# Row divisions and copies on ScalarE for the first batches, sums for several chunks at once, and conversion of whole weight pieces

## The chip, the core and the metric

The kernel runs on one core of a Trainium2 chip. A core has five engines that run their own instruction streams in order and wait for each other by semaphores: TensorE (PE in the profile; its weight loads are PEld), VectorE (DVE), ScalarE (ACT), GpSimd (POOL) and SyncE (SP), which here issues every DMA. The metric is the time of one execution in microseconds on the device; the kernel before takes 2252.2 us (median of 3 runs, 2251.06 to 2255.11).

## The reference

Eight batches of attention, and then one block on the joined heads. For each batch and each of 12 heads (448 tokens, 64 numbers each):

```
q_n, k_n = rmsnorm(q, g_q), rmsnorm(k, g_k)
scores = q_n @ k_n.T / 8;  attn = exp(scores - max);  attn /= sum(attn) + 1e-9
x[:, 64*h : 64*h+64] = attn @ v                     # x: 448 x 768 per batch
u  = x + real(fft(fft(x, axis=tokens), axis=features))
un = (u - mean(u)) / sqrt(var(u) + 1e-6)
out = u + relu(un @ w_ch1) @ w_ch2                  # 768 -> 3072 -> 768
```

All is float32 but for the two weight matrices, which arrive as float64.

## The kernel before

**Stages.** `aux(b)` does the attention of batch b and its Fourier part, `ffn(b)` its feed-forward network (FFN). `aux(0)` runs alone; then, for b = 0 to 7, `ffn(b)` runs merged with `aux(b + 1)`. The generators yield costs and `merge` interleaves them; after that a scheduler of the tile framework settles each engine's order from its own model of the times, so that the order in the built program is not that of the code.

**Attention.** Two heads make a pair, six pairs a batch, and the 448 rows of a pair's scores are four chunks of 112. `softmax_pair` (L325) does for each chunk: scores on TensorE into two PSUM banks (L339 or L342), a minimum per row on VectorE (`mn`; the scores carry a minus sign), the exponential on ScalarE (`P`, with the sum of each row in `sm`), then on VectorE the small operations on `sm` (add 1e-9, reciprocal), and the division of P by its sums, one operation per head: on VectorE, but for head 0 of the first two batches (`EARLY` = 2), where ScalarE does it. `value_pair` (L370) turns P by TensorE transposes, a "remainder" first (`rem`, L374), then three blocks per head (`pt`, L386 or L417), evicts each block from PSUM (`T`) and multiplies it by v (`av`). For the six pairs of batch 0 (`PLAIN_PAIRS`) the eviction is one plain float32 copy, on VectorE and ScalarE in turn; for later pairs it is a split into two parts of the type float32r: ScalarE writes the high part, VectorE the rest. `av` ends in the tile `xT`.

**Fourier part.** `fold` (L472) adds and subtracts halves of xT on VectorE into `eo` and `tot`; matmuls with constant matrices give `y`, ScalarE and VectorE split it into `Y`, and so on up to `un`, whose transposes `unT` are the FFN's input. For batches 2 to 7 the three `eo` of a batch lie in slots of the tag X.

**FFN.** `up(m)` makes 128 of the 3072 hidden rows with 18 matmuls (L844, `h`), `down(g, d)` 128 of the 768 output rows with 12 (L865, `o`). ScalarE and VectorE evict `h` as two float32r parts (`hs`), VectorE adds `o` up in `acc`. Two PSUM banks with the tag ffn serve both.

**Weights.** The matrices come in 60 pieces: 24 of w1 (128 x 768 numbers) and 36 of w2 (128 x 512). Each is turned once from float64 into two float32r parts (`converted`, L682), kept in DRAM, and loaded from there for all later batches. 14 pieces are turned during `aux(0)` (`CONVERT_EARLY`; tiles w1e, w2e), the rest in the FFN of batch 0. `convert` (L632) takes half a piece at a time: a DMA into a raw tile `dbl` (tag X, four slots), two ScalarE operations (L643 `mag`, L644 `dbl`), three on VectorE (L645, L649, L653, all into `mag`), an addition on GpSimd (L657), a cast on ScalarE (L658, `w`) and a subtraction on GpSimd (L659). `mag` is a whole tile for the two halves (tag M, two slots). GpSimd also does the norms' squares, products and powers (`qkn`, `raw`, `ss`) for the early pairs.

`V`, `A` and `G` are recorders, so that most operations of VectorE, ScalarE and GpSimd have the line L111; they are told apart by their tiles.

## Time and profile before

| | |
|---|---|
| three runs | 2252.2, 2251.06, 2255.11 us |
| the profiled execution | 2245.9 us, of which the span from first to last instruction is 2244.1 |
| mean granted TensorE clock | 0.963 |
| TensorE busy (weight loads) | 2107.8 us, 94% (1851.1 us, 82%) |
| VectorE busy | 1636.7 us, 73% |
| ScalarE busy | 1074.1 us, 48% |
| GpSimd busy | 574.0 us, 26% |
| DMA | 425.37 MB, mean 190 GB/s |

The profile is one execution. "Busy" is the time in which an engine has an instruction under way; a matmul's end is modelled, so that a TensorE that is shown as busy all the time need not be at its peak. A row of a group reads: line, engine, operation, tile written <- tiles read, shapes, count | busy us in all, mean ns of one | idle us just before them, and who ended it. A row of the timeline reads: start, duration, engine, line, operation, tiles, shapes, count. The stages follow each other so: attention of batch 0 up to about 150 us, its Fourier part and the handoff to the FFN up to about 200 us, the FFN of batch 0 with the attention of batch 1 up to about 550 us, then the FFNs of batches 1 to 6, each with the attention of the next batch, up to 2000 us, and the last FFN alone.

### The profile page before, as it was taken

The numbers are of one execution on the slowest core, as the hardware profiler recorded it, in microseconds if no ns is written. First come the engines' busy times: TensorE is split into PE (matmuls) and PEld (weight loads), VectorE is DVE, ScalarE is ACT, GpSimd is POOL, SyncE is SP. The second block draws the span as 40 slices with busy tenths as digits, with TensorE's granted clock in tenths as the row PEclk, the third lists the DMA queues.
The fourth block names the chain that finished last, engine by engine and source line by source line (L and its number), as shares of the span: only waits on it lengthen the run. The fifth ranks groups of instructions, "written<-read, shape, count | busy, mean of one in ns | idle before, by whom it ended". The sixth has DMA issues, their size and how long they took to land.

```text
span 2244.1 us, 32060 instructions
## 1 busy us (share of the span) xinstructions
PE 2107.8 (94%) x11164; PEld 1851.1 (82%) x11164; DVE 1636.7 (73%) x3281; ACT 1074.1 (48%) x2452; POOL 574.0 (26%) x442
## 2 busy tenths in 40 slices
PE   6967986788999999999999999999999999999997
PEld 3336865667999999999999999999999999998997
DVE  6897899898688577876788587866788587753122
ACT  5856777475554255534554355524554355422100
POOL 5883567476122011210122021211121022000000
PEclk7997987899999999999999999999999999999999
DMA  5556555577755585556655575557655674539665
GB/s 137 174 167 210 171 171 163 173 266 256 218 174 169 184 238 165 180 182 207 200 171 177 193 222 169 173 177 225 187 171 177 207 215 161 177 132 279 212 215 136
DMA packets 299187, 425.37 MB, mean 190 GB/s; under 512 B 187489, under 2 KB 225362, under 8 KB 299026
## 3 DMA queue, kind: packets, MB, share of 16 engines
q1 hardware_dynamic: 299026, 423.32, 61.1%
q8 instruction: 89, 1.46, 0.3%
q14 instruction: 72, 0.59, 0.1%
HBM read 363.47 MB, written 65.27 MB: 191 GB/s over the span
## 4 chain that ended last, share of the span: by engine, by line
PE 76%; DVE 10%; issue 4%; DMA 3%; POOL 3%; ACT 2%; SPq 0%; DVEq 0%; POOLq 0%; ACTq 0%
PE h L844 28%; PE o L865 27%; PE S L342 5%; PE av L429 4%; PE pt L417 4%; PE y L520 1%; PE qk L305 1%; DVE magw L653 1%; DVE mn L111 1%; DMA dblw<-w 1%; POOL magw L657 1%; DVE magw L645 1%; PE oT L810 1%; DMA u_dram<-u 1%; DMA w<-w 1%
## 5 line engine op out<-in xcount | busy, mean ns | idle before, releaser
L865 PE MATMUL o<-hs,w 128*128 128x448 f32 x3456 | 801.0, 374 | 13.3 <-ACT w L658 4.4
L844 PE MATMUL h<-unT,w 128*128 128x448 f32 x3456 | 781.4, 371 | 3.3 <-DVE hs L111 3.3
L865 PEld LDWEIGHTS o<-hs,w 128*128 128x128 f32 x3456 | 643.9, 191 | 71.7 <-ACT w L658 5.8
L844 PEld LDWEIGHTS h<-unT,w 128*128 128x128 f32 x3456 | 640.5, 189 | 57.1 <-DVE hs L111 4.3
L111 ACT ACTIVATE P<-S,mn 112x448 f32<-112x448 f32 x384 | 243.1, 635 | 218.7 <-DVE mn L111 196.8
L111 POOL TENSOR_TENSOR qkn<-raw 112x1024 f32<-112x1024 f32 x47 | 90.4, 1924 | 740.4 <-PE qk L305 481.2
L111 DVE TENSOR_REDUCE mn<-S 112x1 f32<-112x448 f32 x384 | 232.9, 616 | 48.8 <-PE S L342 45.7
L111 ACT ACTIVATE hs<-h 128x448 fp32r<-128x448 f32 x192 | 104.4, 544 | 294.0 <-PE h L844 293.1
L111 DVE TENSOR_TENSOR acc<-o,acc 128x448 f32<-128x448 f32 x240 | 148.6, 620 | 106.9 <-PE o L865 105.2
L111 DVE SCALAR_TENSOR_TENSOR hs<-h,hs 128x448 fp32r<-128x448 f32 x192 | 119.2, 621 | 125.8 <-ACT hs L111 123.8
L429 PE MATMUL av<-T,vhl 128*128 128x448 f32 x504 | 181.5, 392 | 19.2 <-DVE T L111 12.5
L111 ACT CAST T<-pt 128x448 fp32r<-128x448 f32 x252 | 133.2, 532 | 133.9 <-PE pt L417 131.6
L111 DVE TENSOR_TENSOR T<-pt,T 128x448 fp32r<-128x448 f32 x252 | 154.9, 616 | 35.5 <-ACT T L111 34.0
L111 POOL TENSOR_TENSOR ss<-ss,nhalf 112x16 f32<-112x16 f32 x48 | 151.7, 3160 | 108.9 <-DVE ss L111 107.2
L111 DVE TENSOR_SCALAR P<-P,sm 112x448 f32<-112x448 f32 x336 | 159.5, 509 | 4.3
L342 PE MATMUL S<-KD,QT 128*112 128x448 f32 x352 | 142.6, 407 | 10.5 <-ACT P L111 5.2
L417 PE MATMUL pt<-ident,P 112*128 112x112 f32 x1008 | 147.0, 264 | 4.4 <-DVE R L111 2.8
L417 PEld LDWEIGHTS pt<-ident,P 112*128 112x128 f32 x1008 | 123.0, 143 | 25.7 <-DVE R L111 3.6
L111 POOL TENSOR_TENSOR rstd<-st,nhalf 112x1 f32<-112x1 f32 (+2 forms) x32 | 18.4, 575 | 487.5 <-DVE st L111 484.6
L342 PE MATMUL S<-KL,QT 128*112 128x448 f32 x352 | 134.7, 385 | 2.0 <-DVE KL L111 1.9
L429 PEld LDWEIGHTS av<-T,vhl 128*128 128x128 f32 x504 | 96.4, 192 | 32.0 <-DVE T L111 17.0
L657 POOL TENSOR_TENSOR magw<-magw,dblw 128x256 uint32<-128x256 uint32 (+1 forms) x92 | 87.4, 960 | 81.6 <-DVE magw L653 55.7
(121 smaller groups left out, 2680.3 us busy)
## 6 DMA issues: line engine op xcount, KB each, us to landing
w<-w SPq DMA_DIRECT2D x288, 512.0 KB, 4.3
w<-w SPq DMA_DIRECT2D x192, 768.0 KB, 4.5
dblw<-w SPq DMA_DIRECT2D x60, 256.0 KB, 3.0
dblw<-w SPq DMA_DIRECT2D x32, 384.0 KB, 3.9
raw<-q SPq DMA_DIRECT2D x96, 112.0 KB, 4.6
raw<-k SPq DMA_DIRECT2D x96, 112.0 KB, 3.7
v<-v SPq DMA_DIRECT2D x96, 96.0 KB, 3.6
u_dram<-u SPq DMA_DIRECT2D x24, 336.0 KB, 3.5
```

Of the source, the lines that this page charges most:

```text
L111: ins = emit(*args, **kwargs)
L305: nc.tensor.transpose(pt[:, c * C : (c + 1) * C], qk[:, i, c].rearrange("t h d -> t (h d)"), ident[:C, :C],)
L342: nc.tensor.matmul(s_, QT[:, h, cs], K[:, h], start=step == 0, stop=step == 1)
L417: nc.tensor.transpose(pt[:, c * C : (c + 1) * C], Pc[c][:, 512 * h + j * 128 : 512 * h + (j + 1) * 128], ident[:C, :C],)
L429: nc.tensor.matmul(av[:, :S], lv, T[:, i], start=(j == 0 and i == 0), stop=False)
L520: nc.tensor.matmul(o, src[:, par, t0 : t0 + n], D1[:, ri, par, cols], start=i != 1, stop=i != 0,)
L645: behind(nc.vector.tensor_scalar(out=value, in0=value, scalar1=MIN_HIGH, scalar2=MAX_HIGH, op0=ALU.max, op1=ALU.min,))
L653: behind(nc.vector.scalar_tensor_tensor(out=bits, in0=high, scalar=0xC0000000, in1=bits, op0=ALU.bitwise_and, op1=ALU.bitwise_or,))
L657: behind(nc.gpsimd.tensor_tensor(out=bits, in0=bits, in1=low, op=ALU.add))
L810: nc.tensor.transpose(op[:n, j * 128 : (j + 1) * 128], accs[b][:, 3 * half + j, t0 : t0 + n], ident,)
L844: pace(nc.tensor.matmul(o, w[:, a, c], unT[c][:, z], start=n == 0, stop=n == 17))
L865: pace(nc.tensor.matmul(o, w[:, a, f], hs[4 * g + f][:, z], start=n == 0, stop=n == 11))
```

## The change

Four edits.

1. *Early divisions.* For the first two batches ScalarE does the division for both heads; VectorE keeps those of batches 2 to 7.
2. *Sums of several chunks.* `sm` holds up to four chunks' sums. Adding 1e-9 and the reciprocal are done once for two chunks (batch 0) or four (later batches). The divisions of these chunks come after them, so four or eight in a row.
3. *Plain evictions.* All 36 copies `T` of batch 0 go to ScalarE, where VectorE had 18.
4. *Whole pieces.* `convert` is called once per piece, with a raw tile of 1800 words (two slots in place of four of 900), so each of its operations is twice as wide and there are half as many. Where `fold` used a slot of the tag X, two `eo` now share one wide tile.

```diff
--- before
+++ after
-    SLOTS = {"P": 8, "PT": 6, "X": 4, "M": 2, "unT": 6, "h": 6}
+    SLOTS = {"P": 8, "PT": 6, "M": 2, "unT": 6, "h": 6}
...
+    def wide(name, dtype=F32):
+        return sb.tile([128, 1800], dtype, tag="X", name=name, bufs=2)
...
     def softmax_pair(b, p, Pc):
+        together = 2 if b == 0 else NC
...
-            sm = sb.tile([C, 2], F32, tag="sm", name=f"sm{b}_{p}_{c}", bufs=4)
+            if c % together == 0:
+                sm = sb.tile([C, NC, 2], F32, tag="sm", name=f"sm{b}_{p}_{c}", bufs=2)
...
-                    accum_out=sm[:, h : h + 1],
-                )
-            V.tensor_scalar(
-                out=sm, in0=sm, scalar1=1e-9, scalar2=None, op0=ALU.add
-            )
-            V.reciprocal(sm, sm)
-            for h in range(2):
-                if b < EARLY and h == 0:
-                    A.activation(Ph[h], Ph[h], AF.Copy, scale=sm[:, h : h + 1])
-                    continue
-                V.tensor_scalar(
-                    out=Ph[h], in0=Ph[h], scalar1=sm[:, h : h + 1], scalar2=None,
-                    op0=ALU.mult,
+                    accum_out=sm[:, c % together, h : h + 1],
                 )
             Pc.append(P)
             yield 760
+            if (c + 1) % together:
+                continue
+            sums = sm[:, :together]
+            V.tensor_scalar(
+                out=sums, in0=sums, scalar1=1e-9, scalar2=None, op0=ALU.add
+            )
+            V.reciprocal(sums, sums)
+            for n, P in enumerate(Pc[c + 1 - together : c + 1]):
+                for h in range(2):
+                    ph = P[:, h * S : (h + 1) * S]
+                    if b < EARLY:
+                        A.activation(ph, ph, AF.Copy, scale=sums[:, n, h : h + 1])
+                    else:
+                        V.tensor_scalar(
+                            out=ph, in0=ph, scalar1=sums[:, n, h : h + 1], scalar2=None,
+                            op0=ALU.mult,
+                        )
...
-                    if (h * 3 + j) % 2 == 0:
-                        V.tensor_copy(T, pt[:, :S])
-                    else:
-                        A.copy(T, pt[:, :S])
+                    A.copy(T, pt[:, :S])
...
-        eo = slot(kept, f"eo{b}_{p}").rearrange("r (i t) -> r i t", i=2)
+        if kept is not None:
+            eo = slot(kept, f"eo{b}_{p}")
+        else:
+            if p % 2 == 0:
+                halves[b] = wide(f"eo{b}_{p}")
+            eo = halves[b][:, p % 2 * 900 : p % 2 * 900 + 900]
+        eo = eo.rearrange("r (i t) -> r i t", i=2)
...
-        raw = slot("X", f"dbl{name}", U32)[:, : c * f].rearrange(
+        raw = wide(f"dbl{name}", U32)[:, : c * f].rearrange(
...
-            for c in (slice(0, self.n // 2), slice(self.n // 2, self.n)):
-                convert(
-                    src[:, c], bits[:, c], [hl[:, k, c] for k in range(2)],
-                    f"{self.tag}{name}_{c.start}",
-                )
+            convert(src, bits, [hl[:, k] for k in range(2)], f"{self.tag}{name}")
```

What this does to the order of the instructions, at two places. First VectorE in the steady part, at the end of the last pair (5) of batch 3; a tile's name has batch, pair and chunk (`P3_5_2`: batch 3, pair 5, chunk 2), o2 and acc2 belong to the FFN of batch 2. Before:

```order
L111 TENSOR_REDUCE mn3_5_3_9629<-S3_5_3_0_9631 112x1
L111 TENSOR_REDUCE mn3_5_3_9629<-S3_5_3_1_9632 112x1
L111 TENSOR_TENSOR acc2_7837<-o2_3_0_9645,acc2_7837 128x448
L111 TENSOR_SCALAR sm3_5_3_9630<-sm3_5_3_9630 112x2
L111 RECIPROCAL sm3_5_3_9630<-sm3_5_3_9630 112x2
L111 TENSOR_SCALAR P3_5_3_9628<-P3_5_3_9628,sm3_5_3_9630 112x448 x2
L111 TENSOR_TENSOR T3_4_1_1_9666<-pt3_4_1_1_9661,T3_4_1_1_9666 128x448
L111 TENSOR_TENSOR acc2_7837<-o2_3_1_9671,acc2_7837 128x448
```

And now:

```order
L111 TENSOR_REDUCE mn3_5_3_8825<-S3_5_3_1_8827 112x1
L111 TENSOR_TENSOR acc2_7092<-o2_3_1_8862,acc2_7092 128x448
L111 TENSOR_SCALAR sm3_5_0_8603<-sm3_5_0_8603 112x8
L111 RECIPROCAL sm3_5_0_8603<-sm3_5_0_8603 112x8
L111 TENSOR_SCALAR P3_5_0_8601<-P3_5_0_8601,sm3_5_0_8603 112x448
L111 TENSOR_TENSOR T3_4_1_2_8883<-pt3_4_1_2_8878,T3_4_1_2_8883 128x448
L111 TENSOR_SCALAR P3_5_0_8601<-P3_5_0_8601,sm3_5_0_8603 112x448
L111 TENSOR_SCALAR P3_5_1_8683<-P3_5_1_8683,sm3_5_0_8603 112x448 x2
L111 TENSOR_SCALAR P3_5_2_8763<-P3_5_2_8763,sm3_5_0_8603 112x448 x2
L111 TENSOR_TENSOR KL_66<-qk4_0_1_8888,KD4_0_8814 64x448
L111 TENSOR_SCALAR P3_5_3_8824<-P3_5_3_8824,sm3_5_0_8603 112x448 x2
```

Before, only the last chunk's two divisions come after its minimum, since those of the chunks ahead have been done; now all eight do, and with them work of the FFN (`acc2`) and of the pair ahead (`T3_4`, `KL`) stands among them. On TensorE the order has 27 to 54 matmuls of the FFN between a pair's last scores and the first transpose of its P in batches 3 to 7 (24 to 44 before), and 30 or more in batch 2.

Then ScalarE at the handoff from `aux(0)` to the FFN: `xT0` is the attention's output of batch 0, `xr0` a copy of part of it, `w1e5` and `w1e6` casts of early weight pieces, `dblw2_6` a step of a later piece that waits for its load, `Y0` the evictions of the Fourier part. Before:

```order
L111 COPY xr0_0_1546<-xT0_136 128x6x112
L111 COPY xr0_0_1546<-xT0_136 128x6
L658 CAST w1e5_1379<-magw1e5_1380 128x384 x2
L658 CAST w1e6_1468<-magw1e6_1469 128x384 x2
L111 CAST Y0_0_0_1498<-y0_0_0_1491 113x390
L644 ACTIVATE dblw2_6_0_2205<-dblw2_6_0_2205 128x256
L111 CAST Y0_0_1_1508<-y0_0_1_1501 112x390
L644 ACTIVATE dblw2_6_2_2215<-dblw2_6_2_2215 128x256
L111 CAST Y0_1_0_1518<-y0_1_0_1511 113x390
L111 CAST Y0_1_1_1528<-y0_1_1_1521 112x390
```

And now:

```order
L111 COPY xT0_136<-av0_5_0_1246 64x448
L673 CAST w1e5_1233<-magw1e5_1234 128x768
L111 COPY xT0_136<-av0_5_1_1273 64x448
L111 COPY xT0_136<-xT0_136 128x1
L111 COPY xr0_0_1380<-xT0_136 128x6x112
L111 COPY xr0_0_1380<-xT0_136 128x6
L111 CAST Y0_0_0_1332<-y0_0_0_1325 113x390
L673 CAST w1e6_1312<-magw1e6_1313 128x768
L111 CAST Y0_0_1_1342<-y0_0_1_1335 112x390
L111 CAST Y0_1_0_1352<-y0_1_0_1345 113x390
L111 CAST Y0_1_1_1362<-y0_1_1_1355 112x390
L659 ACTIVATE dblw2_6_2001<-dblw2_6_2001 128x512
```

The cast of `w1e5` has moved from behind both `xr0` copies to between the two last `xT0` copies, that of `w1e6` stands behind the first `Y0`, and the steps of `dblw2_6` no longer stand between the `Y0`. Elsewhere in `aux(0)` and `aux(1)` the order has 48 + 48 divisions on ScalarE (24 + 24 before) and none on VectorE, and 13 of the 14 early pieces pass ScalarE ahead of the first `Y0`, as before.

More of the change, by code (lines that the diff above doesn't have):

```diff
@@ L191, in spectral_block @@
     X_BANKS = (("either", "either"), ("either", "either"))
-    FOLD_SLOTS = (("unT", "unT"), ("PT", "P"), ("M", "X"))
+    FOLD_SLOTS = (("unT", "unT"), ("PT", "P"), ("M", None))
     loaded = {}
@@ L470, in spectral_block @@
     rstds = {}
+    halves = {}
     def fold(b, p, xT, EO):
```

## The prediction

> **What bounds the kernel now.** I read the table by stages first, for which engine is full where, then the chain of waits, then the groups of instructions in the stages that are not full of matmuls. Columns: stretch, length, then busy time of each engine with its count of instructions, granted clock, DMA share, GB/s.
>
> ```profile
> core 0: us, PE busy (x) PEld busy (x) DVE busy (x) ACT busy (x) POOL busy (x), PEclk, DMA share, GB/s
> 25.00:150.00 125.00, 103.84 (x404) 44.84 (x404) 115.98 (x246) 101.99 (x256) 99.52 (x74) 0.91 0.55 165
> 150.00:200.00 50.00, 28.26 (x125) 21.87 (x126) 40.43 (x82) 24.90 (x56) 26.16 (x21) 0.62 0.62 192
> 200.00:250.00 50.00, 50.00 (x277) 45.46 (x276) 35.95 (x73) 36.17 (x84) 20.97 (x18) 1.00 0.51 166
> 250.00:450.00 200.00, 153.71 (x716) 128.60 (x715) 188.78 (x359) 135.22 (x320) 128.37 (x112) 0.83 0.54 173
> 450.00:550.00 100.00, 83.67 (x387) 69.68 (x386) 93.93 (x197) 65.93 (x164) 70.13 (x84) 0.91 0.80 272
> 550.00:2000.00 1450.00, 1448.07 (x8086) 1326.64 (x8086) 1089.74 (x2198) 673.47 (x1510) 219.01 (x122) 1.00 0.62 188
> 2000.00:2244.00 244.00, 227.54 (x1152) 207.96 (x1150) 63.08 (x120) 31.31 (x58) 2.19 (x4) 0.97 0.66 202
> ```
>
> From 550 to 2000 us TensorE is busy 1448 of 1450 us at clock 1.00: only fewer matmuls would shorten it, and the change removes none. The last 244 us hold the last FFN, which the change does not touch. What can move is the first 550 us, where TensorE is not full and its clock falls to 0.83. There VectorE is the full one: 116.0 of 125 us (93%), and 188.8 of 200 (94%). In 450-550 us the DMA engines are busy too (0.80, in one slice 0.86).
>
> ```profile
> PE 76%; DVE 10%; issue 4%; DMA 3%; POOL 3%; ACT 2%; SPq 0%; DVEq 0%; POOLq 0%; ACTq 0%
> 475.00:500.00 25.00, 21.02 (x104) 17.83 (x103) 24.86 (x53) 19.06 (x44) 17.17 (x20) 0.93 0.86 300
> POOL magw L657 <- DVE magw L653: 52.6, 38, 4.3
> ACT dblw L644 <- DMA dblw<-w: 24.6, 21, 4.0
> ```
>
> The chain's 10% on VectorE is 224 us; after 550 us TensorE leaves no room for it. The last two rows are waits between 250 and 550 us: GpSimd waits for VectorE in the conversion, ScalarE for its loads.
>
> **Attention of batch 0 (25-150 us).** VectorE loses its half of the 48 divisions, the 18 evictions and half of the sums' small operations:
>
> ```profile
> L111 DVE TENSOR_SCALAR P<-P,sm 112x448 f32<-112x448 f32 x24 | 17.5, 731 | 0.2
> L111 DVE TENSOR_SCALAR sm<-sm 112x2 f32<-112x2 f32 x24 | 13.1, 547 | 0.0
> L111 DVE COPY T<-pt 128x448 f32<-128x448 f32 x18 | 11.1, 615 | 4.2 <-PE pt L386 4.1
> L111 DVE RECIPROCAL sm<-sm 112x2 f32<-112x2 f32 x24 | 3.7, 154 | 0.1
> ```
>
> That is 17.5 + 11.1 + (13.1 + 3.7)/2 = 37.0 us, so VectorE falls to about 79. ScalarE takes the work over. Its rows of the same operations, and two of the conversion (from 250-450 us):
>
> ```profile
> L111 ACT ACTIVATE P<-P,sm 112x448 f32<-112x448 f32 x24 | 16.1, 672 | 4.0 <-DVE sm L111 3.9
> L111 ACT COPY T<-pt 128x448 f32<-128x448 f32 x18 | 9.5, 529 | 0.1
> L644 ACT ACTIVATE dblw<-dblw 128x384 uint32<-128x384 uint32 x22 | 12.2, 557 | 9.9 <-DMA dblw<-w 9.7
> L644 ACT ACTIVATE dblw<-dblw 128x256 uint32<-128x256 uint32 x26 | 11.1, 435 | 8.3 <-DMA dblw<-w 8.2
> ```
>
> It gains 16.1 + 9.5 us. A whole piece saves it one start per operation: 128 elements cost 557 - 435 = 122 ns, so a whole 512 takes 679 ns where two halves take 870; the 768 saves the same 191 ns. Three operations for each of the 13 pieces that the order has in this stage: 7.4 us. ScalarE comes to 102.0 + 25.6 - 7.4 = 120.2 of 125 us and takes VectorE's place as the full engine. Full without a gap it would allow 120 us (-5); at 85% (TensorE has 83% here now, ScalarE 82%), 141 (+16). I take the 93% that VectorE reaches: 120.2/0.928 = 129.5, **+4 us**.
>
> **The handoff (150-200 us).** Every engine is partly idle; ScalarE by 25 us, in a queue where conversion casts stand ahead of the Y copies. The order puts one cast ahead of the xT copy now and takes a load's wait from between the Y copies. A gain and a loss are both possible; **0**, with 6 us either way (an estimate: a quarter of that idle time). **200-250 us** is full of matmuls: **0**.
>
> **FFN of batch 0 with attention of batch 1 (250-450 us).**
>
> ```profile
> L645 DVE TENSOR_SCALAR magw<-magw 128x384 f32<-128x384 f32 x22 | 14.4, 674 | 0.7 <-ACT magw L643 0.5
> L653 DVE SCALAR_TENSOR_TENSOR magw<-dblw,magw 128x384 uint32<-128x384 uint32 x24 | 14.0, 594 | 0.0
> L111 DVE TENSOR_SCALAR P<-P,sm 112x448 f32<-112x448 f32 x16 | 13.3, 831 | 0.1
> L649 DVE TENSOR_SCALAR magw<-magw 128x256 uint32<-128x256 uint32 x26 | 13.1, 520 | 0.0
> L653 DVE SCALAR_TENSOR_TENSOR magw<-dblw,magw 128x256 uint32<-128x256 uint32 x24 | 12.3, 531 | 0.0
> L649 DVE TENSOR_SCALAR magw<-magw 128x384 uint32<-128x384 uint32 x24 | 12.0, 515 | 0.0
> L645 DVE TENSOR_SCALAR magw<-magw 128x256 f32<-128x256 f32 x26 | 9.2, 371 | 1.1 <-ACT magw L643 1.0
> L111 DVE TENSOR_SCALAR sm<-sm 112x2 f32<-112x2 f32 x16 | 5.2, 324 | 0.0
> ```
>
> The divisions are 13.3 us. The sums are 5.2 us, with reciprocals 16 x 154 ns = 2.5; four chunks at once leave a quarter: -5.8. The six conversion rows make 75.0 us. What of that is work and what is waiting, single rows of the timeline show (VectorE, then two of GpSimd):
>
> ```profile
> 322.26 0.28 DVE L649 TENSOR_SCALAR magw<-magw 128x256 uint32<-128x256 uint32 x1
> 323.40 0.41 DVE L653 SCALAR_TENSOR_TENSOR magw<-dblw,magw 128x256 uint32<-128x256 uint32 x1
> 343.45 0.43 DVE L111 TENSOR_SCALAR P<-P,sm 112x448 f32<-112x448 f32 x1
> 344.73 0.34 DVE L649 TENSOR_SCALAR magw<-magw 128x384 uint32<-128x384 uint32 x1
> 345.52 0.54 DVE L653 SCALAR_TENSOR_TENSOR magw<-dblw,magw 128x384 uint32<-128x384 uint32 x1
> 347.82 3.01 DVE L111 TENSOR_SCALAR P<-P,sm 112x448 f32<-112x448 f32 x1
> 346.64 2.01 POOL L657 TENSOR_TENSOR magw<-magw,dblw 128x384 uint32<-128x384 uint32 x2
> 348.61 1.98 POOL L659 TENSOR_TENSOR w<-magw,w 128x384 fp32r<-128x384 f32 x2
> ```
>
> One division takes 0.43 us, the next 3.01: it ends at 350.83, just as GpSimd's run of four ends at 350.59. The Trainium skill (SBUF — State Buffer, Who interferes with whom) states this as a rule: such a VectorE operation and a GpSimd one share a port pair, and the second waits for the whole instruction of the first. This trace agrees.
>
> Free, three half operations take 0.28 x 2 + 0.41 = 0.97 us (256) or 1.22 us (384). Here some 12.7 pieces of the first and 11.7 of the second kind are 53 us of work and 22 of waiting. By the step from 256 to 384 a whole piece costs 0.40 x 2 + 0.67 = 1.47 or 0.52 x 2 + 0.93 = 1.97 us free: 42 us. Half as many instructions that each wait as long as now add 11: saved 22. If the waits stay 22, 11 is saved; if they go, 33. By the skill's rule each instruction of GpSimd, twice as long, would hold the port twice as long, so the saving would be the 11.
>
> VectorE: 188.8 - 13.3 - 5.8 - 22 = 148 us (137 to 159). ScalarE: 135.2 + 16 x 0.672 - 24.4 x 0.573 = 132. TensorE: 716 matmuls at the pace of 200-250 us (277 in 50) are 129. If VectorE stays 94% full, the stage is 157 us. But ScalarE has nowhere kept more than 82% beside a full engine (102.0 of 125): 132/0.816 = 162, the later of the two: **-38 us** (with VectorE at 159: 168, -32; with VectorE at 137 and 90% full: 152, -48).
>
> **450-550 us.** The same edits act here, but the DMA share is 0.80 with the same bytes to move. At the 0.86 of its fullest slice the stretch takes 93 us: **-6** (0 to -15).
>
> **After 550 us.** From batch 2 on the divisions stay on VectorE but come eight in a row after the fourth chunk, where six came earlier: 6 x 0.43 = 2.6 us later for the transposes of P. What covers this are the FFN matmuls that the order places between a pair's last scores and those transposes, 27 or more. The chain shows their pace, and the length of a batch:
>
> ```profile
> 1243.75 9.75 PE o L865 x48
> 1492.83 9.75 PE o L865 x48
> ```
>
> 27 at 9.75/48 = 0.203 us are 5.5 us, beside 8 x 0.43 = 3.4 us for the run. Cost **0**; without the cover 2.6 us for each of 36 pairs, 94 us.
>
> **The sum.** 4 + 0 + 0 - 38 - 6 + 0 = -40 us. The profiled execution took 2245.9 us (span 2244.1), 6.3 us under the median of 2252.2; it would take 2206, and the median, moved by as much, **2212 us**.
>
> **The rivals.**
>
> *ScalarE becomes the bound (12%).* For it: the 120 of 125 us above, and eight divisions in a row, 8 x 0.67 = 5.4 us, in front of the evictions of batch 1. Against it: in 250-450 us it ends lighter than it was. At 85% in the first stage (+16) and 75% in the second (132/0.75 = 176, -24), with -6: -14, so 2238 us. The Trainium skill (ScalarE: Activation LUTs, Rules for kernel authors) speaks for this: it wants multiplications on VectorE, not ScalarE. The trace bears it out only where GpSimd is quiet: 0.67 us against 0.43 free, but against 0.83 on average here.
>
> *VectorE was the only brake (10%).* With 94% kept at 137 us of work, 250-450 us shrinks by 55, 450-550 by 15, the first stage by 5: -75, or -65 with 450-550 us held at -5 by its DMA: 2187 us.
>
> *The conversion loop, slower (7%).* Two pieces are in flight (two raw tiles, two M tiles). A whole piece no longer overlaps its own halves. A load of that size and GpSimd's part:
>
> ```profile
> w<-w SPq DMA_DIRECT2D x288, 512.0 KB, 4.3
> L657 POOL TENSOR_TENSOR magw<-magw,dblw 128x384 uint32<-128x384 uint32 x24 | 27.7, 1166 | 31.6 <-DVE magw L653 23.0 <-DVE sm L111 5.2 <-issue 3.4
> ```
>
> A piece takes 200/24.4 = 8.2 us now, so 16.4 from load to release. Its steps add up to 4.3 + 2 x 0.68 + 1.47 + 2 x 1.2 + 0.6 = 10.1; without overlap of halves, half of that, 5.1, is added. For it: the 24.6 us of waits for loads. Against it: most of the 16.4 us is waiting for a full VectorE, which is what goes. It decides where the waits per piece fall by less than 5.1 us: if by 4, each of the 37 pieces that fall between 250 and 550 us at this pace costs 1.1/2 us, +20: 2272 us.
>
> *The loop and the lighter VectorE cancel (8%):* no change, 2250 us. *The run of eight divisions is exposed (3%):* past 40/36 = 1.1 us per pair it turns the gain into a loss; at 2 us, 2284 us.
>
> That the change doesn't do what it says is out: the order has all 96 early divisions on ScalarE.
>
> **The numbers.** Forecast 60%, 2212 us. The range holds it and the cases on both sides of it up to no change: 2182 to 2249. Faster by over 0.2% (4.5 us, about what a measurement of this kernel can tell): 0.60 + 0.12 + 0.10 = 0.82; within it 0.08; slower 0.07 + 0.03 = 0.10.
>
> **What would show it.** Right: TensorE becomes full some 40 us earlier than at 550; VectorE under 93% and ScalarE over 93% in the first stage; the mean of the early tensor_scalars nearer to 0.43; from then on the same 1492.8 - 1243.8 = 249 us per batch. Wrong: ScalarE with idle time for VectorE still in the first stage, loads at the head of the waits of 250-550 us, or TensorE with gaps at P's transposes after 550 us.

## The result: 33 us slower, and the profile after

The changed kernel takes 2285.1 us (median of 4 runs, 2279.0 to 2288.0) beside 2251.6 for the kernel before (4 runs, 2248.8 to 2255.1) on the same chip: a ratio of 1.0144, 95% interval 1.0118 to 1.0171. The forecast was 2212. The profiled execution after took 2288.0 us, of which its span is 2286.2. The table by stages, in the stretches of before, with the same columns:

```profile
core 0: us, PE busy (x) PEld busy (x) DVE busy (x) ACT busy (x) POOL busy (x), PEclk, DMA share, GB/s
25.00:150.00 125.00, 102.16 (x365) 43.68 (x366) 77.64 (x131) 107.87 (x243) 81.99 (x48) 0.83 0.49 150
150.00:200.00 50.00, 30.84 (x136) 20.88 (x135) 37.82 (x65) 24.98 (x46) 24.62 (x15) 0.70 0.51 152
200.00:250.00 50.00, 48.29 (x254) 43.09 (x252) 27.83 (x52) 37.30 (x83) 13.81 (x11) 0.94 0.66 220
250.00:450.00 200.00, 152.29 (x719) 128.27 (x718) 176.46 (x252) 142.60 (x281) 117.31 (x69) 0.88 0.54 177
450.00:550.00 100.00, 84.94 (x397) 72.93 (x397) 70.39 (x124) 56.62 (x106) 55.45 (x40) 0.87 0.73 256
550.00:2000.00 1450.00, 1426.80 (x7881) 1296.24 (x7880) 1071.29 (x1953) 663.79 (x1495) 229.37 (x126) 1.00 0.60 185
```

VectorE was relieved: 116 to 78 us in the first stage, 189 to 176 between 250 and 450 (148 was forecast), 94 to 70 between 450 and 550. TensorE gained nothing from it: 152.3 us between 250 and 450 where it had 153.7, 719 matmuls where it had 716. In the first stage it is busy as long as before (102.2 and 103.8 us), but does 365 matmuls in that time instead of 404, at a granted clock of 0.83 instead of 0.91. And from 550 to 2000 us, where it had been full, it now stands still for 23 us and does 205 matmuls fewer. The shares of the chain say whom it waits for; TensorE had 76%, VectorE 10%, DMA 3%:

```profile
PE 65%; DVE 14%; DMA 8%; ACT 6%; issue 3%; POOL 3%; SPq 1%; POOLq 0%; DVEq 0%; ACTq 0%
```

The time of the first `y` matmul of each batch, from the timeline, parts the execution into stages that belong to the work. Here are all the kernels told of below. "Twice" is the kernel before, profiled a second time. The fourth column is a fifth of the time from the first y of batch 2 to that of batch 7. These three columns are of one profiled execution each. The ratio is that of the medians to the kernel before on the same chip, which took 2251.6 to 2255.4 us there.

| kernel | y of batch 0 | from there to y of batch 2 | one batch, 2 to 7 | time, us | ratio, 95% interval |
|---|---|---|---|---|---|
| before | 156.3 | 598.9 | 248.0 | | |
| before, twice | 156.5 | 601.8 | 248.3 | | |
| after | 174.8 | 598.5 | 253.8 | 2285.1 | 1.0118 to 1.0171 |
| late divisions per chunk | 171.8 | 597.2 | 248.2 | 2255.3 | 0.9985 to 1.0014 |
| halves again | 182.1 | 591.7 | 253.9 | 2287.8 | 1.0111 to 1.0159 |
| sums alone | 167.4 | 582.6 | 254.2 | 2268.4 | 1.0034 to 1.0065 |
| whole pieces alone | 167.3 | 594.9 | 247.7 | 2254.4 | 0.9975 to 1.0004 |
| late runs of four | 170.8 | 596.5 | 248.5 | 2257.1 | 1.0002 to 1.0039 |
| late other operation | 172.4 | 607.5 | 258.9 | 2322.2 | 1.0282 to 1.0338 |
| quiet GpSimd | 169.6 | 596.7 | 251.2 | 2271.7 | 1.0052 to 1.0107 |
| divisions alone | 182.2 | 587.0 | 248.0 | 2261.1 | 1.0024 to 1.0058 |
| evictions alone | 164.8 | 592.1 | 248.0 | 2247.6 | 0.9958 to 0.9992 |
| no VectorE in conversion | 159.1 | 521.4 | 247.9 | 2170.3 | 0.9609 to 0.9655 |
| ScalarE only in conversion | 155.6 | 487.5 | 247.9 | 2126.1 | 0.9407 to 0.9460 |
| VectorE aside | 187.0 | 607.4 | 248.1 | 2287.3 | 1.0123 to 1.0174 |
| three raw tiles | 181.6 | 605.6 | 247.6 | 2274.4 | 1.0058 to 1.0116 |
| VectorE whole, others halves | 166.6 | 602.9 | 247.8 | 2258.2 | 1.0004 to 1.0029 |
| sums of batch 1 alone | 169.7 | 585.1 | 248.2 | 2248.2 | 0.9949 to 0.9985 |
| evictions + sums of batch 1 | 167.0 | 583.0 | 247.8 | 2244.7 | 0.9953 to 0.9979 |
| the same + divisions of batch 1 | 167.8 | 585.4 | 247.7 | 2243.1 | 0.9947 to 0.9976 |

In the changed kernel the first y comes 18.5 us later, the middle is as long as before (598.5 and 598.9), and five batches take 1269.0 us where they took 1240.1, 28.9 more. So of the forecast of -40 us, +4 became some +18, -44 became nothing, and 0 became +29. The rest of the difference between the two profiled executions lies behind the y of batch 7, where two executions of the kernel before differ by some 4 us (248.8 and 252.5 us) and the changed kernel's took 243.9.

### The profile page after: what moved, and what is told of

The parts are those of the page before. It is cut to its first block, busy times and chain, and to the rows that moved or that the text cites. A ratio compares the mean times of both kernels' runs of the same rounds, so it can differ in the third digit from the quotient of the medians.

```text
span 2286.2 us, 31151 instructions
## 1 busy us (share of the span) xinstructions
PE 2127.4 (93%) x11164; PEld 1857.2 (81%) x11164; DVE 1564.0 (68%) x2759; ACT 1080.2 (47%) x2338; POOL 532.4 (23%) x322
## 4 chain that ended last, share of the span: by engine, by line
PE 65%; DVE 14%; DMA 8%; ACT 6%; issue 3%; POOL 3%; SPq 1%; POOLq 0%; DVEq 0%; ACTq 0%
PE o L876 23%; PE h L855 23%; PE S L347 5%; PE av L436 4%; PE pt L424 3%; ACT P L111 3%; DVE P L111 2%; DMA w<-w 2%; DMA dblw<-w 2%; DMA u_dram<-u 2%; PE y L535 1%; DVE magw L668 1%; PE qk L308 1%; DVE mn L111 1%; DVE eo L111 1%
## 5 line engine op out<-in xcount | busy, mean ns | idle before, releaser
L855 PE MATMUL h<-unT,w 128*128 128x448 f32 x3456 | 790.3, 372 | 9.6 <-DVE hs L111 3.9
L111 DVE TENSOR_REDUCE mn<-S 112x1 f32<-112x448 f32 x384 | 234.4, 618 | 96.2 <-PE S L347 83.7
L111 ACT CAST T<-pt 128x448 fp32r<-128x448 f32 x252 | 132.7, 532 | 103.8 <-PE pt L424 102.4
L436 PE MATMUL av<-T,vhl 128*128 128x448 f32 x504 | 174.6, 387 | 6.4 <-DVE xT L111 2.7
L111 DVE TENSOR_SCALAR P<-P,sm 112x448 f32<-112x448 f32 x288 | 150.6, 586 | 0.9
L672 POOL TENSOR_TENSOR magw<-magw,dblw 128x512 uint32<-128x512 uint32 (+1 forms) x46 | 69.9, 1520 | 81.5 <-DVE magw L668 57.4
```

The source lines that it names most:

```text
L111: ins = emit(*args, **kwargs)
L436: nc.tensor.matmul(av[:, :S], lv, T[:, i], start=(j == 0 and i == 0), stop=False)
L672: behind(nc.gpsimd.tensor_tensor(out=bits, in0=bits, in1=low, op=ALU.add))
L855: pace(nc.tensor.matmul(o, w[:, a, c], unT[c][:, z], start=n == 0, stop=n == 17))
```

## The experiments

### The late batches: is it the run of eight?

*Late divisions per chunk.* In the changed kernel, batches 2 to 7 go back to one chunk at a time, with four tiles for the sums and the yield behind the divisions as before.

```diff
-        together = 2 if b == 0 else NC
+        together = (2, NC, 1)[min(b, 2)]
```

> The changed kernel with the sums and divisions of batches 2 to 7 per chunk again, two divisions at a time, as in the kernel before; batches 0 and 1 stay changed. Theory 1, the run of eight: in batches 2 to 7 eight divisions in a row meet the operations of GpSimd and hold back the additions into acc and the subtractions of hs behind them; then batches 2 to 7 go back to 249 us each, 29 us less than in the changed kernel, and with part of the 11 us between the first y of batch 1 and of batch 2 the time is 2245 to 2258 us. Theory 2, another part (the shared wide tile of eo, or the order of the loads) slows the batches: still about 254 us per batch, 2280 to 2290.

2255.3 us, 248 us per batch as before, and the profile lists no wait of TensorE between 755 and 2050 us. In the changed kernel these were its largest waits there (us in all, times, longest):

```profile
PE o L876 <- DVE acc L111: 4.0, 4, 1.3
PE o L876 <- DVE hs L111: 2.1, 2, 1.1
PE h L855 <- DVE hs L111: 1.6, 5, 0.5
PE o L876 <- ACT acc L111: 1.4, 3, 0.6
```

So some 30 us are the late sums' doing, and the other parts of the change together come to nothing (ratio 0.9985 to 1.0014). The waits name what stands behind the divisions on VectorE (`acc`, `hs`), but they are only half of the loss. Before and after:

```profile
1000.00:2000.00 1000.00, 999.90 (x5603) 916.65 (x5602) 749.19 (x1518) 464.03 (x1040) 144.73 (x82) 1.00 0.61 187
1000.00:2000.00 1000.00, 988.49 (x5474) 897.42 (x5473) 735.84 (x1344) 457.22 (x1028) 146.72 (x82) 1.00 0.60 185
```

TensorE is idle for 11.5 of these 1000 us, but does 129 matmuls fewer, which are 23 us at the pace of before. The other half lies in time in which it is shown as busy. One reason is that a matmul is shown with some 0.36 us while the next follows it by 0.20, so that the first 0.16 us of a wait count as busy. How a run of eight does it can be read from one of batch 3's. VectorE:

```profile
1085.64 0.20 DVE L111 RECIPROCAL sm<-sm 112x8 f32<-112x8 f32 x1
1085.88 5.67 DVE L111 TENSOR_SCALAR P<-P,sm 112x448 f32<-112x448 f32 x8
1091.47 0.61 DVE L111 SCALAR_TENSOR_TENSOR hs<-h,hs 128x448 fp32r<-128x448 f32 x1
...
1119.47 2.97 DVE L111 TENSOR_SCALAR P<-P,sm 112x448 f32<-112x448 f32 x8
```

GpSimd meanwhile, with the squares of the next pair's q and k and the scaling of its k:

```profile
1087.57 1.96 POOL L111 TENSOR_TENSOR qkn<-raw 112x1024 f32<-112x1024 f32 x1 [16.14 <-PE qk L308]
1089.61 1.33 POOL L111 TENSOR_TENSOR raw<-raw,gneg 112x512 f32<-112x512 f32 x1
```

And TensorE in that stretch:

```profile
PE h L855 <- DVE hs L111: 0.5, 1, 0.5
```

Eight free divisions take 3.0 us, as the next run of this batch, which meets nothing. This one took 5.67: two of its divisions lasted 2.09 and 1.48 us, about as long as GpSimd's two operations. `hs` stood behind it, and its PSUM bank and TensorE behind `hs`. A second way is longer. The run at 1176.74 met both operations too and ended 6.35 us later; the reduction of the next pair's squares came late behind it, GpSimd's power after that, and VectorE, which needs that power, stood still with the next `hs` in its queue:

```profile
1190.19 1.29 DVE L111 TENSOR_TENSOR qkn<-raw,ss 112x512 f32<-112x512 f32 x2 [0.83 <-POOL ss L111]
1191.41 0.61 DVE L111 TENSOR_REDUCE mn<-S 112x1 f32<-112x448 f32 x1
1191.94 0.61 DVE L111 SCALAR_TENSOR_TENSOR hs<-h,hs 128x448 fp32r<-128x448 f32 x1
```

```profile
1192.61 1.07 PE L876 MATMUL o<-hs,w 128*128 128x448 f32 x4 [1.07 <-DVE hs L111]
```

Of the 30 runs of the steady part, nine took up to 3.52 us, and no gap of TensorE over 0.1 us stands within 4 us of their ends; three of them met the end of the shorter GpSimd operation. 21 took 4.5 to 6.4, and nine of these have such a gap.

*Sums alone.* The kernel before with the second edit only; head 0's early divisions stay the only ones on ScalarE.

```diff
+        together = 2 if b == 0 else NC
...
+            for n, P in enumerate(Pc[c + 1 - together : c + 1]):
...
+                    if b < EARLY and h == 0:
```

> The kernel before with the sums of two and four chunks at once and nothing else. Theory 1, the run of eight slows batches 2 to 7: 254 us per batch, 2275 to 2285 us. Theory 2, it does not: 249 us per batch, 2240 to 2252.

254 us per batch, as theory 1 has it, but 2268.4 us: the stretch from the first y of batch 0 to that of batch 2 became 16 us shorter (582.6), which I hadn't expected. That stretch starts 11 us later here, so 5 us are left at the y of batch 2. Merged sums cost late; that they gain early is tested below, for batch 1.

*Late runs of four.*

```diff
-        together = 2 if b == 0 else NC
+        together = 2 if b != 1 else NC
```

> The changed kernel with the sums of batches 2 to 7 over two chunks instead of four, so that four divisions come in a row, twice a pair. Theory 1 (the eight in a row hold back what stands behind them on VectorE, the more the longer the run): 251 us per batch or less, 2257 to 2270 us. If any merging of sums across chunks costs the same, whatever the length of the run: 254 us per batch, 2280 to 2290.

248.5 us per batch. None of the 60 runs of four from 755 us on meets one of the two GpSimd operations. The mean of a division, from 755 to 2000 us, is the measure of the meetings; the changed kernel, then this one:

```profile
L111 DVE TENSOR_SCALAR P<-P,sm 112x448 f32<-112x448 f32 x232 | 126.0, 604 | 0.8
```

```profile
L111 DVE TENSOR_SCALAR P<-P,sm 112x448 f32<-112x448 f32 x240 | 92.8, 448 | 1.6
```

*Late other operation.* The changed kernel, its late divisions by scalar_tensor_tensor (each call on one line here).

```diff
-                        V.tensor_scalar(out=ph, in0=ph, scalar1=sums[...], scalar2=None, op0=ALU.mult)
+                        V.scalar_tensor_tensor(out=ph, in0=ph, scalar=sums[...], in1=ph, op0=ALU.mult, op1=ALU.min)
```

> The changed kernel with the divisions of batches 2 to 7 by scalar_tensor_tensor (times the reciprocal, then the minimum with P itself, which changes no value as the reciprocal is below 1). In the traces scalar_tensor_tensor takes 0.62 us for such a tile beside any GpSimd work, the tensor_scalar 0.44 when GpSimd is quiet and up to 2.1 beside it. Theory 1a, the meetings with GpSimd make the run of eight harmful (it takes 5 to 6.4 us where GpSimd is busy): each run is now 5.0 us whatever GpSimd does, the worst runs go, and the batch falls to 250 to 252 us, 2260 to 2275 in all. Theory 1b, the place and the length of the run do it: 5.0 us instead of a mean of about 4.7, no better, 254 to 256 us per batch, 2285 to 2298.

Slower still, 2322.2 us, 258.9 per batch, but its premise fell too. One run on VectorE, then GpSimd in it:

```profile
837.49 7.54 DVE L111 SCALAR_TENSOR_TENSOR P<-P,sm 112x448 f32<-112x448 f32 x8
844.95 0.61 DVE L111 SCALAR_TENSOR_TENSOR hs<-h,hs 128x448 fp32r<-128x448 f32 x1
```

```profile
839.36 2.36 POOL L111 TENSOR_TENSOR qkn<-raw 112x1024 f32<-112x1024 f32 x1 [16.49 <-PE qk L308]
841.80 1.56 POOL L111 TENSOR_TENSOR raw<-raw,gneg 112x512 f32<-112x512 f32 x1
```

The operation takes 0.68 us free and meets GpSimd all the same (one division of such a run lasted 2.32 us). I had taken `hs` for a sample of it, but `hs` has only one of its inputs in SBUF, these divisions have two. The Trainium skill (SBUF — State Buffer, Who interferes with whom) says just that: a VectorE instruction with two SBUF inputs contends with a GpSimd instruction that reads SBUF. The traces agree. So this run doesn't part meetings from length; it shows that longer runs (4.9 to 8.1 us) lose more, 10.9 us per batch.

*Quiet GpSimd.* The changed kernel, with those two GpSimd operations moved away from batch 2 on.

```diff
-        (G if nth else V).tensor_tensor(out=sq, in0=flat, in1=flat, op=ALU.mult)
+        if b < EARLY:
+            (G if nth else V).tensor_tensor(out=sq, in0=flat, in1=flat, op=ALU.mult)
+        else:
+            A.activation(sq, flat, AF.Square)
...
-        (G if nth else V).tensor_tensor(
+        (G if 0 < nth < EARLY * NPAIR else V).tensor_tensor(
             out=kf, in0=kf, in1=gneg[:, None, :].broadcast_to([C, 8, D]), op=ALU.mult
```

> The changed kernel with two of GpSimd's operations per pair taken off it from batch 2 on: the squares of q and k go to ScalarE, the scaling of k to VectorE. The runs of eight stay. In the changed kernel the nine runs that met neither operation took 3.0 to 3.5 us and no gap of TensorE stands near them; the gaps stand near runs of 4.5 us and more, which met them. Theory 1a, the meetings make the harm: every run takes 3.0 to 3.5 us, a batch 249 to 251 us, the total 2255 to 2267. Theory 1b, eight in a row do harm by their place and number alone: 253 to 255 us per batch, 2278 to 2290.

2271.7 us, between the two: 13 of the 30 us are back. The runs are quiet now, and no gap stands near one:

```profile
L111 DVE TENSOR_SCALAR P<-P,sm 112x448 f32<-112x448 f32 x240 | 90.8, 445 | 0.7
```

The waits of TensorE for VectorE are gone. What is left, between 760 and 2040 us, is above all for ScalarE:

```profile
PE h L858 <- ACT unT L111: 4.4, 5, 1.3
PE S L350 <- ACT P L111: 1.8, 3, 0.8
PE o L879 <- ACT acc L111: 1.4, 3, 0.5
```

ScalarE has the squares here, so part of these are this kernel's own price; how much, no run parts. With the meetings 13 us went, which is strong evidence that they make the run harmful; but the edit also moves work and changes the order, and for the rest of the 30 us it isn't shown.

### The first 560 us: why was there no gain?

*Whole pieces alone*, the kernel before with the fourth edit only, and *halves again*, the changed kernel without it (the same lines the other way).

```diff
-        raw = slot("X", f"dbl{name}", U32)[:, : c * f].rearrange(
+        raw = wide(f"dbl{name}", U32)[:, : c * f].rearrange(
...
-            for c in (slice(0, self.n // 2), slice(self.n // 2, self.n)):
...
+            convert(src, bits, [hl[:, k] for k in range(2)], f"{self.tag}{name}")
```

> The kernel before with whole pieces per conversion and the wide tile, and nothing else. Theory 3, whole pieces save time between 250 and 450 us and cost nothing elsewhere: 2225 to 2245 us, 249 us per batch. Theory 4, two whole pieces in flight cost time up to the first y of batch 0: that y comes at about 175 us, the time is 2255 to 2270. Theory 2, the shared tile slows the late batches: 254 us per batch, 2275 or more.

> The changed kernel with the conversion in halves again (four raw tiles of 900, eo in a slot of its own). Theory 3, the conversion of whole pieces saves VectorE's time and the ScalarE edits cost the 18 us before the first y of batch 0: the time gets worse, 2295 to 2310, and the first y of batch 0 stays at about 175 us. Theory 4, the loop of whole pieces costs the 18 us: the first y of batch 0 falls to about 157 us and the time to about 2267. Under theory 2 the batches 2 to 7 also go back to 249 us, which gives 2240 to 2258.

Neither way does it matter (2254.4 beside 2255.4; 2287.8 beside 2285.1). The edit does relieve VectorE; whole pieces alone:

```profile
250.00:450.00 200.00, 152.04 (x715) 127.69 (x714) 187.05 (x285) 126.16 (x246) 115.29 (x67) 0.85 0.52 171
450.00:550.00 100.00, 80.07 (x370) 68.58 (x370) 75.95 (x136) 56.97 (x107) 57.57 (x41) 0.88 0.74 259
```

Between 450 and 550 us VectorE has 24 us to spare, and TensorE is no fuller than before. So a full VectorE isn't what holds TensorE there. Between 250 and 450 us VectorE stays full: its six conversion rows fall from 75.0 to 55.9 us, but the 16 divisions there take 18.7 us (13.3 before) and the 16 additions to the sums 10.6 (5.2), beside GpSimd instructions of twice the length. The pace of the conversion stays too. By the trace, ScalarE's first step was done for 48 halves in this stretch before, and for 24 whole pieces with this edit; from that step to GpSimd's last a half took 13.4 us and a whole piece takes 13.5. Four halves were in between for 51% of the time, two pieces are for 69%.

TensorE's own waits for converted pieces (`w`) between 250 and 550 us were 5.7 us before and are 18.0 with whole pieces alone; in the changed kernel they are 16.7, with halves again 5.6. The largest, before and in the changed kernel:

```profile
PE o L865 <- ACT w L658: 4.4, 3, 2.8
PE o L876 <- ACT w L673: 9.4, 5, 3.4
```

All its waits there come to 62 us in both of these kernels. So whole pieces come later to TensorE, by about as much as its other waits shrink.

*No VectorE in conversion* leaves out VectorE's three operations of the conversion; *ScalarE only* leaves out GpSimd's and the cast too, and lets two ScalarE operations write the parts. In both, and in the kernel after them, the weights lack what these steps do.

```diff
-        behind(nc.vector.tensor_scalar(
-            out=value, in0=value, scalar1=MIN_HIGH, scalar2=MAX_HIGH,
...
-        behind(nc.vector.tensor_scalar(
-            out=bits, in0=bits, scalar1=5, scalar2=2,
...
-        behind(nc.vector.scalar_tensor_tensor(
-            out=bits, in0=high, scalar=0xC0000000, in1=bits,
...
```

```diff
...
+        behind(nc.scalar.activation(part[0], high.bitcast(F32), AF.Abs))
+        behind(nc.scalar.activation(part[1], high.bitcast(F32), AF.Abs))
```

> The kernel before without the three VectorE operations of the conversion (the weights come out without clamping, shift and sign). It takes 144 us of busy time from VectorE between 160 and 560 us and three steps from each piece's chain. If VectorE or the chain of a piece is the brake there, the time falls by 40 to 100 us, to 2150 to 2210. If neither is (loads, GpSimd, TensorE's clock), less than 15 us: 2237 or more.

> The kernel before with the conversion cut to two ScalarE operations per half, which write the two parts straight from the raw tile; VectorE, GpSimd and the third ScalarE operation are left out (the weights come out wrong). If VectorE alone is the brake of the first 550 us, it gains no more than the run without its operations: 2155 to 2172. If the chain or GpSimd is part of it, 2100 to 2145.

82 and 126 us less. So the conversion does set the pace of this stretch. Without VectorE's steps a half takes 6.9 us, 76 are started between 250 and 450 us (48 before), and TensorE is full from 450:

```profile
250.00:450.00 200.00, 178.18 (x923) 152.91 (x922) 145.62 (x248) 166.98 (x413) 166.30 (x167) 0.97 0.79 260
450.00:550.00 100.00, 99.07 (x548) 90.09 (x547) 73.79 (x142) 54.95 (x136) 28.33 (x29) 1.00 0.74 241
```

GpSimd's part and the cast are worth another 44 us, though VectorE is busy for only 146 of 200 us in the kernel that still has them: the brake is more than a full VectorE. Part of the gain is TensorE's clock, which was 0.83 and 0.91 in these two stretches and is 0.97 and 1.00. By these shares the same matmuls need some 37 us less (an estimate: 0.14 of 200 us and 0.09 of 100), and no run tells whether the fuller TensorE is the reason.

*VectorE aside.* The three operations stay, at their size, on a tile that nobody reads.

```diff
-            out=value, in0=value, scalar1=MIN_HIGH, scalar2=MAX_HIGH,
+            out=side, in0=high.bitcast(F32), scalar1=MIN_HIGH, scalar2=MAX_HIGH,
...
-            out=bits, in0=bits, scalar1=5, scalar2=2,
+            out=sideb, in0=sideb, scalar1=5, scalar2=2,
...
-            out=bits, in0=high, scalar=0xC0000000, in1=bits,
+            out=sideb, in0=high, scalar=0xC0000000, in1=sideb,
```

> The kernel before with the three VectorE operations of the conversion kept at their size, but on a tile of their own that nothing reads, so that a piece's chain goes from ScalarE straight to GpSimd (the weights come out without clamping, shift and sign). Without these operations at all the time was 2170, 82 us less. If VectorE's occupation is the brake (theory 5), leaving them out of the chain gains little: 2235 to 2255. If the length of the chain with two pieces in flight is the brake (theory 6), most of the 82 us is gained: 2170 to 2195.

2287.3 us, which neither theory has. Two of the three operations still read the raw tile and so hold its slot, and the order put these operations early (110.5 of 125 us of VectorE before 150 us, with 335 matmuls on TensorE where it had 404). Of its 35 us, 31 stand before the first y of batch 0. It decides nothing on the question.

*Three raw tiles.*

```diff
-    SLOTS = {"P": 8, "PT": 6, "X": 4, "M": 2, "unT": 6, "h": 6}
+    SLOTS = {"P": 8, "PT": 6, "X": 3, "M": 2, "unT": 6, "h": 6}
```

> The kernel before with three raw tiles instead of four, nothing else. In its trace 3.4 of 4 halves are on average between ScalarE's first and GpSimd's last operation, each for 11.1 us, and 52 are started between 200 and 450 us. Theory 6, the chain with so many in flight sets the pace: with three the pace falls to about 3/4, some 40 halves in that stretch, the conversion ends at 610 us or later instead of 551, the total is 2300 to 2350. Theory 5, VectorE's occupation sets the pace: the halves queue less and each takes less time, at most 20 us are lost, 2252 to 2272.

21 us slower, at the edge of theory 5 and far from the size that theory 6 gave; the conversion ends at 582 us, not at 610. And most of it isn't in the stretch that was asked about: the first y of batch 0 comes 25 us later, the middle is 7 us longer. Between 250 and 450 us a half takes 11.0 us instead of 13.4, and 44 are started instead of 48. (The expectation's 11.1 us are the mean over 200 to 550 us.) With fewer in flight each half goes faster and the pace falls by 8%, not by a quarter: there the halves mostly queue, as theory 5 has it, and three or four tiles make little difference. It speaks against the number of raw tiles as the brake; what they queue for it doesn't tell. More tiles would be the other half of the test; it wasn't run.

*VectorE whole, others halves.* Whole loads and VectorE operations; ScalarE and GpSimd work on each half in turn.

```diff
+        for h in parts:
+            behind(nc.scalar.activation(value[:, h], high[:, h].bitcast(F32), AF.Abs))
+            behind(nc.scalar.activation(low[:, h], low[:, h], AF.Copy, scale=2.0**-29))
...
+        for h in parts:
+            behind(nc.gpsimd.tensor_tensor(
+                out=bits[:, h], in0=bits[:, h], in1=low[:, h], op=ALU.add
```

> The kernel before with the wide tile and whole pieces for the loads and VectorE's three operations, but ScalarE's and GpSimd's operations in halves as before. If the twice as long instructions of GpSimd give back what whole pieces save VectorE (its divisions took 0.91 us on average with whole pieces alone, 0.74 before, its sums' additions 0.60 instead of 0.32), they go, and the time is 2230 to 2245. If the chain with two raw tiles in flight sets the pace, the time is that of whole pieces alone, 2250 to 2260.

2258.2 us: halving ScalarE's and GpSimd's instructions does not bring the gain back. It isn't a clean test of their length, though: between 250 and 450 us a division takes 0.67 us on average (1.17 with whole pieces alone, 0.83 before), but an addition to the sums 0.90 (0.66, 0.32 before), and VectorE is as busy as ever (187 of 200 us).

*Before, twice*, *divisions alone* and *evictions alone* (the kernel before with the first edit only, and with the third).

```diff
-                if b < EARLY and h == 0:
+                if b < EARLY:
```

```diff
-                    if (h * 3 + j) % 2 == 0:
-                        V.tensor_copy(T, pt[:, :S])
-                    else:
-                        A.copy(T, pt[:, :S])
+                    A.copy(T, pt[:, :S])
```

> The kernel before, unchanged, profiled a second time, as a measure of how much one profile's stages vary. If the first y of batch 0 comes at 156 us again (within 3) and the end at 2244, the 11 to 18 us by which it is later in the changed kernel and in the runs with one part alone are the edits' doing. If it comes at 160 to 170 and the end nearer to 2250, most of that is the spread of single executions, and no step may be judged by it.

> The kernel before with all early divisions on ScalarE and nothing else. If VectorE's occupation is the brake, the 30.8 us of divisions that leave it (17.5 and 13.3) shorten the first 450 us by 5 to 20: 2232 to 2248. If the chain is, ScalarE's later casts cost as much: 2248 to 2262.

> The kernel before with all 36 copies of T of batch 0 on ScalarE and nothing else. If ScalarE lies on the chain of attention of batch 0 (its exponentials, and what each edit adds to it), the first y of batch 0 comes 5 to 15 us later and the time is 2254 to 2264. If VectorE is the brake there, its 11 us less make it earlier or equal: 2242 to 2252.

The kernel before repeats its 156 us, but its end comes at 2252.5, not at 2244: 3 us of that lie in the middle and 4 behind the y of batch 7. So one profile's total is known to some 8 us only. The divisions alone cost 8.6 us, which is the chain's side of the expectation, and bring the first y 26 us later; the middle gets 12 us shorter. What stands in front of TensorE's `av` in the first stage is no longer VectorE's copy `T` but ScalarE's, which wait behind divisions. Divisions alone, up to 185 us, and the kernel before, up to 160 us:

```profile
PE av L396 <- ACT T L111: 10.5, 7, 3.1
```

```profile
PE av L396 <- DVE T L111: 9.1, 5, 2.4
```

These two waits are of nearly the same size, so they don't make the 26 us. From 25 us to the first y, TensorE does some 410 matmuls in each kernel. It is busy with them for 104.8 us before, at a mean clock of 0.90, and for 122.2 with the divisions alone, at 0.77; its idle time there grows by 8 us only, from 26.5 to 35. The changed kernel lies between: 116.3 us at 0.81, idle for 33.5. So the larger part of the delay is slower matmuls at a lower granted clock. Why the clock is lower, whether for the waits or for another reason, no run shows.

The evictions alone gain 6 us, though their first y is 8.5 us later.

*Sums of batch 1 alone*, and two kernels that put together what gained: this with the evictions, and the two with the divisions of batch 1.

```diff
+        together = NC if b == 1 else 1
```

```diff
-                    if b < EARLY and h == 0:
+                    if b == 1 or (b < EARLY and h == 0):
```

> The kernel before with the sums of four chunks at once in batch 1 alone. With the sums alone everywhere, the first y of batch 0 came 11 us later, and the stretches from there to that of batch 1 and on to that of batch 2 were 7 and 9 us shorter. If these belong to the batches in which the sums are merged, this kernel keeps the 156 us and gains 7 to 16: 2236 to 2246. If they are only two orders of the same work, 2248 to 2258.

> The kernel before with two parts of the change: all T copies of batch 0 on ScalarE, and the sums of four chunks at once in batch 1 only. Alone they took 2247.6 and 2248.2 beside 2253.8 for the kernel before, 6 us less each. If the gains are of different stages and add up: 2238 to 2245. If each is only another order of a stage that is paced by the chain of the conversion: 2245 to 2254.

> The same with all divisions of batch 1 on ScalarE too; those of batch 0 stay half and half. If the 8.6 us that the divisions on ScalarE cost alone lie in batch 0, where its first y came 26 us later and the two stretches after it were 6 us shorter each, this kernel is 3 to 12 us faster than the one without. If they cost in both batches, as ScalarE also converts, it is 0 to 10 us slower than that.

The sums of batch 1 alone gain 5.5 us, and with the evictions 8.4 (2244.7, ratio 0.9953 to 0.9979): a kernel that beats both. The divisions of batch 1 beside them change nothing that can be told (2243.1), so the loss of the first edit should be batch 0's, whose divisions weren't run by themselves. One warning came with it: in the kernel with the sums of batch 1 alone the code of batch 0 is the old one, yet its first y came at 169.7 us. Up to there its TensorE is idle for 29.3 us (26.5 before), but busy for 115.4 with the same 410 matmuls, at a clock of 0.82. So that point moves by some 13 us with the granted clock, with no edit to its code; whether a new order by the scheduler lowers the clock isn't known. The 8 to 18 us by which other kernels are late there therefore say little of their edits. The 26 of the divisions are twice that.

The stages also trade with each other. The first three edits alone shorten the middle by 12, 16 and 7 us, but each starts it 8 to 26 us later; together in the changed kernel they start it 18.5 us later and shorten it by nothing. Why their gains don't add up there, no run shows.

## The steps of the prediction

**"25-150 us: +4."** VectorE's 79 us were right (77.6). ScalarE was to be 93% full and was 86% (107.9 of 125), and TensorE did 365 matmuls where it did 404. The first y came 18.5 us later, near the rival's +16 at 85%. But the mechanism is not the rival's, or not for the most part: I looked for TensorE's time in waits, and its busy time hardly changed (103.8 and 102.2 us). A matmul took 0.257 us of it before and 0.280 after, as the clock went from 0.91 to 0.83. I had no term for the clock. The page's rule that I gave for the rival (the Trainium skill, ScalarE: Activation LUTs, Rules for kernel authors: multiplications to VectorE) agrees with the divisions alone, which lose 8.6 us; for those of batch 1 nothing can be told.

**"150-200 and 200-250 us: 0."** Between these clock times little changed (28.3 to 30.8, 50.0 to 48.3 us of TensorE), though other work now falls there.

**"250-450 us: -38", "450-550 us: -6".** This step failed: the middle took 598.5 us instead of 598.9. Two things in it. VectorE came to 176.5 us, not to 148, and ScalarE to 142.6, not 132. The conversion in this stretch, by its six rows:

```profile
L668 DVE SCALAR_TENSOR_TENSOR magw<-dblw,magw 128x768 uint32<-128x768 uint32 x11 | 15.2, 1386 | 0.0
L664 DVE TENSOR_SCALAR magw<-magw 128x768 uint32<-128x768 uint32 x11 | 11.3, 1025 | 0.1
L660 DVE TENSOR_SCALAR magw<-magw 128x768 f32<-128x768 f32 x12 | 10.8, 900 | 4.0 <-ACT magw L658 4.0
L668 DVE SCALAR_TENSOR_TENSOR magw<-dblw,magw 128x512 uint32<-128x512 uint32 x13 | 10.4, 801 | 0.2
L664 DVE TENSOR_SCALAR magw<-magw 128x512 uint32<-128x512 uint32 x13 | 9.4, 723 | 0.3
L660 DVE TENSOR_SCALAR magw<-magw 128x512 f32<-128x512 f32 x13 | 7.3, 565 | 3.5 <-ACT magw L658 3.4
```

That is 64.4 us, 10.6 less than the 75.0 before, not 22 less: the lower bound of 11, which was the one by the rule of the Trainium skill (SBUF — State Buffer, Who interferes with whom) that the second waits for the first's whole instruction. It doesn't confirm the rule: with whole pieces alone the same rows came to 55.9, which is 19 less, and the waiting turned up in the divisions and additions. The divisions went as forecast (13.3); the small operations on the sums saved 3.8 of 5.8, and the rest of the room was taken by other work and waits. The graver error is the other one: the step took VectorE, being 94% full, for what sets the stage's length. At 88% of the first stretch and 70% of the second TensorE did no more than before. VectorE works and waits inside a chain; the waits of 250 to 550 us show the chain after the change:

```profile
POOL magw L672 <- DVE magw L668: 57.4, 29, 7.4
POOL w L674 <- ACT w L673: 36.8, 24, 4.4
DVE magw L660 <- ACT magw L658: 27.2, 19, 3.2
```

GpSimd's wait for VectorE is as long as ever (52.6 before), and VectorE now waits for ScalarE too. The rival "the loop and the lighter VectorE cancel" (8%) has the number of the kernel without the late runs: 2255.3 us, no change. Of its mechanism there is a part: TensorE's waits for pieces grew by 11 us and its others shrank by as much. But with halves again, where pieces come no later, the y of batch 2 comes at 773.8 us, as in the changed kernel (773.3). So this is not the whole account, and the number is in part luck. The "-6" rested on the DMA share of 0.80; it fell to 0.73, and TensorE's busy time stayed at 84.9 us (83.7).

**"After 550 us: 0."** This failed too, and is the 30 us of the result: the term was put at nothing, and the late runs of eight cost 29 us. I asked whether the transposes of P were covered; they are (TensorE waits for P some 0.7 us in all there). I didn't ask who is queued behind the run on VectorE, and priced its divisions at the free 0.43 us, though the prediction itself quotes one of 3.01 that met GpSimd. It was the 3% rival in sign and place, but not by the wait for P that it names; its price, 29 us over 30 runs of the steady part, is 1 us each, near the 1.1 at which it said the gain would be gone. But no gain stood against it.

**What is open.** Three candidates are left for what sets the length of the middle, and no run parts them: VectorE's occupation, the chain of a piece, and TensorE's clock. Shown is that relieving VectorE by 12 us of 200 and by 24 of 100 brought nothing, that the fourth raw tile is worth some 7 us there, and that leaving out VectorE's steps of the conversion, occupation and chain together, brings 82 us. For the late runs, half of the 30 us is not tied to the meetings with GpSimd.

## What to carry to other kernels

Of an engine that is 94% busy, ask what it is busy with: inside a chain with few buffers, half as many instructions of twice the length left the pace as it was. Before operations are gathered into a run, read what stands behind them in that engine's queue, and what another engine does meanwhile that lengthens them; four in a row cost nothing here, eight 30 us. And look at the granted clock before calling a later point a wait: here it moved an early one by 13 us with no edit to its code. Compare where stages have met again.

## What the runs showed of the hardware

A free VectorE division of 112x448 takes 0.44 us and, in the late batches, lasts up to 2.09 beside a GpSimd operation on SBUF, about as long as that operation (1.9 to 2.1 us). GpSimd's power of 112x16 (3.4 us beside a run at 703 us) did not lengthen a run. scalar_tensor_tensor with both inputs in SBUF took 0.68 us free and up to 2.32 beside the same operations. TensorE's time per matmul followed its granted clock: between 25 and 150 us 0.257 us at 0.91, 0.280 at 0.83, and 0.297 at 0.79 with the divisions alone (345 matmuls in 102.6 us).
